# Expert layer by halves of the output, a last pair in two chains, and several steps of the plan moved

## The chip, the cores and the metric

The kernel runs on one core of a Trainium2 chip. The metric is the device time of one execution in microseconds. A NeuronCore has TensorE (PE, its weight loads shown as PEld), VectorE (DVE), ScalarE (ACT), GpSimd (POOL) and SyncE (SP), which here issues most of the DMAs. Matmuls write to PSUM (banks of 128 x 512 float32); ScalarE or VectorE copy from there to SBUF.

## The reference

Three layers, one after the other, on 8 batches of 576 tokens with 8 heads of 64, so 4608 tokens of 512:

```python
kv = einsum('bhsd,bhse->bhde', k, v)
out = einsum('bhsd,bhde->bhse', q, kv)
out = out / sqrt(mean(out * out, -1) + 1e-6) * g_norm      # linear attention, x = [4608, 512]

h = x @ w_in                                               # [4608, 2048]
x = (h * cos(h)) @ w_out                                   # [4608, 512]

logits = x @ phi                                           # [4608, 32]: 8 experts of 4 slots
d = softmax of logits over the tokens                      # slot_input = d.T @ x
slot_out[e] = relu(slot_input[e] @ w1[e]) @ w2[e]          # 512 -> 1024 -> 512, 8 experts
return (softmax of logits over the slots) @ slot_out       # [4608, 512]
```

## The kernel before

**Blocks.** The tokens are cut into ten blocks (`SIZES`, L64): blocks 0 to 7 of 512 and blocks 8 and 9 of 256 tokens. For each block j and each of 16 slices f of the hidden layer, `main(j, f)` (L382) makes one PSUM bank `h` with 12 matmuls: the weights and the inputs are split in a high and a low part, and three of the four products are taken. `h * cos(h)` follows in four steps: `turns` (ScalarE, L406), `rest` (VectorE, L409), the cosine (ScalarE, L413) and the product (VectorE, L443), which leaves `gT`. There are three `h` banks. Blocks 8 and 9 put two slices of 256 columns in one bank and run these four steps once for the pair (L1114).

**Logits and slots.** `w_out` isn't multiplied out: `wp = w_out @ phi` is made in four parts (`wp_kk`, `wp_tr`, L332 to L348), and the logits are `wp` times `gT` (`logits`, and `logits2` for pairs of slices in blocks 0 and 1). `gT` is also brought into the other orientation, by TensorE transposes (`gtr`) or by VectorE transposes and DMAs (`regroup`), and multiplied with the softmax weights `d` (`slot_acc`, L612). For block 9 the end of this is a chain: `l_add` (L544, the last slices' part of the logits), `l_max`, `l_exp` (L563), `l_T` (transposes of `ld`, copy to `d`), `last_slots`.

**The next block's inputs.** While block n runs, the inputs of block n + 1 are made in its steps, per tile t of 128 tokens: `att_out` (matmuls, square, reduction, a power on POOL), `att_xs` (scaling), `att_xT` (transposes, copy `hi` on ScalarE) and `att_lo` (the remainder `lo` on VectorE, L253). The first `main` of a block needs all of its tiles.

**The plan.** The order of each engine's work is written out by hand. `at(j, f, fn)` puts a call behind `main(j, f)` (list `side`), `late` behind `rest` (list `post`), `end` behind the product (`fin`), `ld_at` ahead of the step (`loads`). `at2` counts on from one block into the next. Blocks 0 and 1 run interleaved (`L=4`: slice f of block 0 with slice f - 4 of block 1; string `PLAN["two"]`): `s0 m0 ... m1 ... s1`, so what is put at (0, f) runs ahead of `main(0, f)`, and what is put at (1, f - 4) runs behind `main(1, f - 4)` in the same step. In these steps the weights are still being converted (L300 to L326). `PLAN["A"]` gives the steps of `att_out`, `att_xs`, `att_xT` and `att_lo` for the next block.

**The experts.** w1 and w2 are loaded by `fill` calls into buffers as these come free (`todo`, L661, is the order: all of w1, w2 of experts 0 to 3 in 512 columns, then w2 of experts 4 to 7 as two halves of 256 columns). `tail` (L739) makes the slot inputs, then `first_layer(0)` and `(1)` for the two groups of four experts, `h_T`, and the second layer: `second_layer(0)` for group 0 in 512 columns, `second_layer(1, 1)` and `second_layer(1, 2)` for the two halves of group 1. Its loop has eight steps r of four matmuls, and `then` puts calls behind a step. Once a half of the columns is there for both groups, `select` arranges it, and `half_out(h, u)` (u from 0 to 5) multiplies it with the token weights `cT` (made by `c_T(j)`, j from 0 to 11, two per `half_out`), copies three banks and issues an output DMA of 768 KB on SP. The buffers of the last six refills (`w13` to `w15`, in the list `mid`) hold the last rows of w1 and the first rows of w2 of experts 0 and 1 until then.

## Time and profile before

| | us |
|---|---|
| median of 3 runs | 690.12 (689.81 to 691.18) |
| the profiled execution | 689.97 |
| its span, first to last instruction | 688.2 |
| PE busy | 655.5 (95%) |
| VectorE busy | 496.9 (72%) |
| ScalarE busy | 332.2 (48%) |
| mean granted clock of TensorE | 0.987 |

A line of the timeline gives the start and the duration of an instruction, or of several alike that follow each other (x24), and in brackets how long its engine had been idle and what ended that. Matmuls are pipelined, so one ends after the next has begun; for the time that PE spends, starts are compared with starts. A float32 matmul shows as two instructions. The clock is given as a share of 2.4 GHz: 1.00 and 0.50 are its two levels, and a value in between is a mean over a stretch that has both.

### The profile page before, as it was taken

The page shows a single profiled execution, that of the slowest core. Times are in us where ns is not written, and L with a number is a line of the kernel's source. Part 1 is how long each engine was busy: PE and PEld are TensorE (multiplying, and loading weights), DVE is VectorE, ACT ScalarE, POOL GpSimd, SP SyncE. Part 2 cuts the span into 40 slices and gives each one's busy share as a digit, 9 for nine tenths or more (in the row PEclk, how much of TensorE's full clock was granted, in tenths as well). Part 3 has the DMA queues.
Part 4 walks back from the last instruction along what each step waited for, and adds up shares of the span by engine and source line. Part 5 has one row for each costly group of instructions (what it writes and reads, how often), then busy time and mean ns, then how long its engine had stood idle before and what let it go on. Part 6 is the DMA issues. An engine that isn't in the chain of part 4 may idle for free.

```text
span 688.2 us, 12481 instructions
## 1 busy us (share of the span) xinstructions
PE 655.5 (95%) x4556; PEld 481.2 (70%) x4556; DVE 496.9 (72%) x893; ACT 332.2 (48%) x587; POOL 218.1 (32%) x329
## 2 busy tenths in 40 slices
PE   6879999999999999999999999999999999989994
PEld 6767776875667776767677677767767778874364
DVE  3899987966577778878887888788876656444153
ACT  3675764644354454445445544553554354551143
POOL 3361111211074343540633253245324505001400
PEclk9999999999999999999999999999999999999995
DMA  9945562112186636784777277486635459999978
GB/s 327 363 155 183 198 220 94 57 62 77 51 204 156 172 77 169 202 238 118 167 214 211 70 193 231 120 225 168 150 94 116 103 165 352 334 403 406 373 288 345
DMA packets 72893, 135.12 MB, mean 196 GB/s; under 512 B 11008, under 2 KB 38784, under 8 KB 72320
## 3 DMA queue, kind: packets, MB, share of 16 engines
q1 hardware_dynamic: 65664, 119.63, 54.1%
q0 software_dynamic: 7168, 14.69, 9.1%
q8 instruction: 36, 0.59, 0.4%
q14 instruction: 25, 0.20, 0.1%
HBM read 91.29 MB, written 13.63 MB: 152 GB/s over the span
## 4 chain that ended last, share of the span: by engine, by line
PE 81%; DVE 8%; ACT 5%; issue 2%; DMA 2%; POOL 1%; SPq 0%; DVEq 0%; ACTq 0%; POOLq 0%
PE h L390 50%; PE ab L612 4%; PE ops L203 4%; PE l L515 4%; PE kvps L184 2%; PE eo L792 2%; PE eh L765 2%; PE xTps L240 2%; PE l L524 2%; PE fo L817 2%; PE tr L484 1%; DVE gT L443 1%; ACT tmp L413 1%; PE lr L540 1%; DMA kv<-in_kv 1%
## 5 line engine op out<-in xcount | busy, mean ns | idle before, releaser
L390 PE MATMUL h<-xt,w 128*128 128x512 f32 (+1 forms) x1920 | 422.0, 374 | 6.5 <-DVE xt L253 2.7
L390 PEld LDWEIGHTS h<-xt,w 128*128 128x128 f32 x1920 | 330.1, 189 | 92.1 <-issue 15.2
L413 ACT ACTIVATE tmp<-tmp,hpi 128x512 f32<-128x512 f32 x144 | 104.0, 723 | 174.3 <-DVE tmp L409 174.2
L503 POOL DMA_DIRECT2D g<-tr x224 | 123.4, 554 | 95.5 <-DVE tr L462 50.2
L443 DVE TENSOR_TENSOR gT<-tmp,h 128x512 f32<-128x512 f32 x131 | 89.8, 686 | 70.6 <-ACT tmp L413 70.5
L215 POOL TENSOR_TENSOR ri<-ss,mhalf 128x8 f32<-128x8 f32 x36 | 59.6, 1660 | 210.2 <-DVE ss L213 205.3
L409 DVE SCALAR_TENSOR_TENSOR tmp<-h,tmp 128x512 f32<-128x512 f32 x144 | 97.0, 677 | 22.8 <-ACT tmp L406 22.1
L406 ACT ACTIVATE tmp<-h 128x512 int32<-128x512 f32 x144 | 85.0, 590 | 51.0 <-PE h L390 50.8
L462 DVE STREAM_TRANSPOSE tr<-gT 128x512 f32<-128x512 f32 x103 | 73.3, 711 | 6.4 <-DMA g<-tr 1.6
L326 POOL TENSOR_TENSOR w<-st_m,w 128x512 fp32r<-128x512 f32 x16 | 21.4, 1338 | 72.1 <-ACT w L321 72.1
L203 PE MATMUL ops<-kvA,q 128*128 128x128 f32 (+1 forms) x320 | 38.4, 279 | 0.0
L244 ACT ACTIVATE xt<-xTps,gn 128x512 fp32r<-128x512 f32 x36 | 24.4, 683 | 28.3 <-PE xTps L240 28.3
L203 PEld LDWEIGHTS ops<-kvA,q 128*128 128x128 f32 (+1 forms) x320 | 34.4, 180 | 3.0 <-issue 2.2
L253 DVE SCALAR_TENSOR_TENSOR xt<-xTps,gn,xt 128x512 fp32r<-128x512 f32 x36 | 26.1, 730 | 7.6 <-ACT xt L244 7.3
L210 ACT ACTIVATE sq<-ops 128x512 f32<-128x512 f32 x32 | 19.0, 595 | 25.6 <-PE ops L203 25.3
L612 PE MATMUL ab<-g,d 128*32 128x512 f32 x256 | 31.3, 593 | 0.0
L515 PE MATMUL l<-gT,wp 128*32 128x512 f32 (+1 forms) x248 | 30.2, 556 | 0.0
L212 DVE TENSOR_REDUCE ss<-sq 128x8 f32<-128x512 f32 x32 | 21.6, 675 | 8.0 <-ACT sq L210 7.8
L184 PEld LDWEIGHTS kvps<-kv 128*64 128x64 f32 x448 | 15.4, 137 | 11.7 <-issue 8.7
L222 DVE TENSOR_TENSOR sq<-ops,ri 128x512 f32<-128x512 f32 x32 | 21.5, 677 | 2.3 <-POOL ri L215 2.3
L240 PE MATMUL xTps<-ident,sq 128*128 128x128 f32 x128 | 19.7, 278 | 3.4 <-DVE sq L222 3.4
L612 PEld LDWEIGHTS ab<-g,d 128*32 128x32 f32 x256 | 8.9, 110 | 18.6 <-issue 16.8
(184 smaller groups left out, 633.6 us busy)
## 6 DMA issues: line engine op xcount, KB each, us to landing
kv<-in_kv SPq DMA_DIRECT2D x28, 512.0 KB, 5.3
g<-tr SPq DMA_DIRECT2D x224, 64.0 KB, 3.6
g<-tr POOLq DMA_DIRECT2D x224, 64.0 KB, 3.8
q<-in_qT SPq DMA_DIRECT2D x36, 256.0 KB, 5.9
out<-ot SPq DMA_DIRECT2D x12, 768.0 KB, 4.1
ew<-in_w SPq DMA_DIRECT2D x17, 512.0 KB, 10.3
rw<-in_w_in SPq DMA_DIRECT2D x16, 512.0 KB, 4.4
nat<-in_w_out SPq DMA_DIRECT2D x16, 512.0 KB, 3.9
```

Of the source, the lines that this page charges most:

```text
L203: nc.tensor.matmul(out=ps[p0:p0 + n, pr * 128:(pr + 1) * 128], lhsT=q_t[j, t][:, pr, p0:p0 + n], rhs=kvbd[b % 2][:, pr, :], start=True, st ...
L215: nc.gpsimd.tensor_tensor(out=ri[:, :, 0], in0=ss, in1=mhalf, op=ALU.pow)
L240: nc.tensor.transpose(ps[:, kk * 128:(kk + 1) * 128], xs[:, kk * 128:(kk + 1) * 128], ident)
L390: nc.tensor.matmul(out=ps, lhsT=w[:, a, kk, :], rhs=x[b][:, kk, :], start=(n == 0), stop=(n == 3 * KD - 1))
L406: nc.scalar.activation(out=t.bitcast(I32), in_=ps, func=AF.Copy, bias=0.25, scale=INV_2PI)
L409: nc.vector.scalar_tensor_tensor(out=t, in0=ps, scalar=INV_2PI, in1=t.bitcast(I32), op0=ALU.mult, op1=ALU.subtract)
L413: nc.scalar.activation(out=t, in_=t, func=AF.Sin, bias=hpi, scale=TWO_PI)
L443: nc.vector.tensor_tensor(out=g, in0=fr, in1=h_t.pop((j, f)), op=ALU.mult)
L462: nc.vector.transpose(out=tr_t[j, q][:, :, i, :], in_=gT_t[j, n * q + i].rearrange("p (b t) -> p b t", t=32))
L503: (nc.gpsimd if b % 2 else nc.sync).dma_start(out=dst[32 * b:32 * b + 32, :, x, a:a + n, :].rearrange("p t f i -> p t (f i)"), in_=src[32 ...
L515: nc.tensor.matmul(out=l_t[j][32 * o:32 * o + 32, :], lhsT=wp[:, f, :], rhs=gT_t.pop((j, f)), start=(c == 0), stop=(c == (2 if j == NB - 1 ...
L612: nc.tensor.matmul(out=ps[32 * c:32 * c + 32, :], lhsT=d[:, t, :], rhs=gs[c // 2][t][:, (c % 2) * 512:(c % 2) * 512 + 512], start=(t == 0) ...
```

## The change

In the plan of block 1, `att_out` of block 2's third and fourth tile goes from steps 12 and 13 to 11 and 12, their `att_xT` from 14 and 15 to 13 and 14. In block 8, the second tile of block 9 has its `att_xT` in step 13 instead of 15. `logits2(1, 4)` goes from (0, 11) to (1, 7), and `logits2(1, 12)` from (1, 15) to (1, 17), which is (2, 1). The last pair of slices of block 9 gets two banks and two chains of 256 columns. The copy of the raw logits for the token weights goes from `l_exp` to `l_T`, `l_raw` to just before `c_softmax`. The second layer runs group 0 in halves too: half 1 of both groups, then half 2 of group 0 with two `half_out` in it, then half 2 of group 1 with two more. The very last output goes out in three DMAs of 256 KB.

```diff
--- before.py
+++ after.py
@@ -48,7 +48,7 @@
     lT=20,
     sa=22,
     A=(((1, 1, 2, 2), (1, 1, 1, 1), (2, 2, 3, 3), (0, 1, 1, 0)),
-       ((9, 10, 12, 13), (0, 0, 0, 0), (11, 12, 14, 15), (0, 0, 0, 0))),
+       ((9, 10, 11, 12), (0, 0, 0, 0), (11, 12, 13, 14), (0, 0, 0, 0))),
     K=((0, (0, 0, 0, 0)), (1, (1, 3, 5, 7)), (1, (13, 15, 17, 19))),
     KL=(((0, 1), (1, 2), (1, 4), (1, 6)), ((1, 11), (1, 14), (1, 16), (2, 2))),
     ao=(2, 5, 8, 11),
@@ -396,7 +396,7 @@
 
     def exp_table():
         t = sm_p.tile([128, 2], F32, tag="sb", name="et")
-        nc.scalar.activation(out=t[:, 0:1], in_=m_run, func=AF.Exp, scale=0.0)
+        nc.scalar.activation(out=t[:, 0:1], in_=mhalf[:, 0:1], func=AF.Exp, scale=0.0)
 
     def cos_a(j, f):
         fr_tt(j, f)
@@ -417,7 +417,7 @@
         return tmps[tmp_n[0] % 2]
 
     def fr_tt(j, f):
-        fr_t[j, f] = tmp_one()
+        fr_t[j, f] = tmp_one()[:, 0:h_t[j, f].shape[-1]]
         turns(fr_t[j, f], h_t[j, f])
 
     def round_off(j, f):
@@ -437,9 +437,18 @@
         ring.append([(j, f)] + r[1:])
         return r[1]
 
+    last_g = []
+
     def cos_c(j, f):
         fr = fr_t.pop((j, f))
-        g = ring_next(j, f)
+        g = last_g.pop() if last_g else ring_next(j, f)
+        if (j, f) in ((NB - 1, NF - 2), (NB - 1, NF - 1)):
+            if f % 2 == 0:
+                last_g.append(g[:, 256:512])
+                g = g[:, 0:256]
+            gT_t[j, f] = g
+            nc.vector.tensor_tensor(out=g, in0=fr, in1=h_t.pop((j, f)), op=ALU.mult)
+            return
         nc.vector.tensor_tensor(out=g, in0=fr, in1=h_t.pop((j, f)), op=ALU.mult)
         if j >= SMALL:
             gT_t[j, f], gT_t[j, f + 1] = g[:, 0:256], g[:, 256:512]
@@ -562,9 +571,7 @@
         sb = sm_p.tile([128, 2], F32, tag="sb", name="sb")
         nc.scalar.activation(out=ld, in_=ps, func=AF.Exp, bias=mb[:, 2:3], accum_out=sb[:, 0:1])
         if j == NB - 1:
-            lraw = we[:, 512:512 + SIZES[j]]
-            nc.vector.tensor_copy(out=lraw[0:32], in_=ps[0:32])
-            ls_t[j] = lraw
+            ls_t[j] = ps
         else:
             nc.vector.tensor_copy(out=ld[0:32], in_=ps[0:32])
         if j:
@@ -588,7 +595,11 @@
         nc.vector.tensor_copy(out=d, in_=ps[:, 0:TT[j], 32:64])
         if not tok:
             tok.append(const.tile([128, NT, NS], F32, tag="l_tok", name="l_tok"))
-        if j < NB - 1:
+        if j == NB - 1:
+            lraw = we[:, 512:512 + SIZES[j]]
+            nc.vector.tensor_copy(out=lraw[0:32], in_=ls_t[j][0:32])
+            ls_t[j] = lraw
+        else:
             nc.vector.tensor_copy(out=tok[0][:, T0[j]:T0[j] + TT[j], :], in_=ps[:, 0:TT[j], 0:32])
         d_t[j] = d
 
@@ -784,17 +795,17 @@
         so = [a_p.tile([128, 512], F32, tag="a", name="so") for _ in range(2)]
         st_all = one_p.tile([128, 2, 256], F32R, tag="ls", name="st")
 
-        def second_layer(G, h=0, then={}):
-            n = 256 if h else 512
-            ps = (at_bank("eo") if h == 2 else ps_m.tile([128, 512], F32, tag="h", name="eo"))[:, 0:n]
+        def second_layer(G, h, then={}):
+            ps = (at_bank("eo") if h == 2 else ps_m.tile([128, 512], F32, tag="h", name="eo"))[:, 0:256]
+            c = (h - 1) * 256
             for r in range(8):
                 for i in range(4):
+                    w = GR[i, 1, 0, r][:, c:c + 256] if G == 0 else GR.pop((4 + i, 1, h, r))
                     nc.tensor.matmul(out=ps[32 * i:32 * i + 32, :], lhsT=hT[G][0][:, r, 32 * i:32 * i + 32],
-                                     rhs=GR.pop((4 * G + i, 1, h, r)), start=(r == 0), stop=(r == 7))
+                                     rhs=w, start=(r == 0), stop=(r == 7))
                 for fn, *a in then.get(r, ()):
                     fn(*a)
-            c = max(h - 1, 0) * 256
-            nc.scalar.copy(out=so[G][:, c:c + n], in_=ps)
+            nc.scalar.copy(out=so[G][:, c:c + 256], in_=ps)
 
         def select(h):
             cc = slice(256 * (h - 1), 256 * h)
@@ -817,12 +828,17 @@
                     nc.tensor.matmul(out=ps[:, 256 * x:256 * x + 256], lhsT=cT_t[j][0:96, t, :], rhs=st[0:96],
                                      start=True, stop=True)
                 (nc.vector.tensor_copy if (3 * u + v) % 2 else nc.scalar.copy)(out=ot[:, 512 * v:512 * v + 512], in_=ps)
-            nc.sync.dma_start(out=out[h - 1, u], in_=ot.rearrange("p (q c) -> p q c", c=256))
+                if (h, u) == (2, 5):
+                    nc.sync.dma_start(out=out[1, 5, :, 2 * v:2 * v + 2],
+                                      in_=ot[:, 512 * v:512 * v + 512].rearrange("p (q c) -> p q c", c=256))
+            if (h, u) != (2, 5):
+                nc.sync.dma_start(out=out[h - 1, u], in_=ot.rearrange("p (q c) -> p q c", c=256))
 
         def two(pool, tag):
             t = pool.tile([128, 2, 1536], F32, tag=tag, name="ot")
             return [t[:, 0], t[:, 1]]
 
+        l_raw(NB - 1)
         c_softmax()
         first_layer(0)
         relu(0)
@@ -840,19 +856,18 @@
         h_T(0, 0)
         h_T(0, 1)
         c_T(0)
-        second_layer(0, then={0: [(c_T, 1)], 1: [(h_T, 1, 0)], 3: [(h_T, 1, 1)]})
-        second_layer(1, 1)
+        second_layer(0, 1, then={0: [(c_T, 1)], 1: [(h_T, 1, 0)], 3: [(h_T, 1, 1)], 5: [(c_T, 2)], 7: [(c_T, 3)]})
+        second_layer(1, 1, then={3: [(c_T, 4)]})
         half = {1: (select(1), two(g_p, "g1") + [gt_p.tile([128, 1536], F32, tag=f"gt{i}", name="ot") for i in (1, 0)]
                     + two(g_p, "g0"))}
-        for u in range(2):
-            c_T(2 * u + 2)
-            c_T(2 * u + 3)
-            half_out(1, u)
-        second_layer(1, 2, then={2: [(c_T, 6), (c_T, 7), (half_out, 1, 2)], 5: [(c_T, 8), (c_T, 9), (half_out, 1, 3)]})
+        second_layer(0, 2, then={2: [(half_out, 1, 0)], 6: [(half_out, 1, 1)]})
+        for j in range(5, 8):
+            c_T(j)
+        second_layer(1, 2, then={0: [(half_out, 1, 2)], 3: [(c_T, 8)], 4: [(half_out, 1, 3)], 6: [(c_T, 9)]})
         half[2] = (select(2), [t_p.tile([128, 1536], F32, tag="T2", name="ot")] + two(g_p, "g1")
                    + [gt_p.tile([128, 1536], F32, tag="gt1", name="ot")] + two(g_p, "g0"))
+        c_T(10)
         half_out(1, 4)
-        c_T(10)
         c_T(11)
         half_out(1, 5)
         for u in range(6):
@@ -916,7 +931,12 @@
         if j < 2:
             for f in range(0, NF, 2):
                 late_in = j and f + 3 + L >= NF - (L < 6)
-                at2(*((1, f + 3) if late_in else (0, max(f + 3 + L, 9) if j else PLAN["l0"][f // 2])), logits2, j, f)
+                if not j:
+                    at2(0, PLAN["l0"][f // 2], logits2, j, f)
+                elif f == 4 or late_in:
+                    at2(1, 17 if f == 12 else f + 3, logits2, j, f)
+                else:
+                    at2(0, max(f + 3 + L, 9), logits2, j, f)
         if j < NB - 1:
             for c in range(4 * (j > 1)):
                 at2(j, 4 * c + 7 if j == SMALL else PLAN["lg"][c], logits, j, c)
@@ -944,8 +964,6 @@
         at2(j, lT, l_T, j)
         at2(j, sa, slot_acc, j)
         end2(j, sa, slot_add, j)
-        if j == NB - 1:
-            at2(j, sa, l_raw, j)
 
     for b in range(1, B):
         p, i = divmod(b, 2)
@@ -961,7 +979,7 @@
         if n < 2:
             ao, dx, xt, dl = PLAN["A"][n]
         elif n == SMALL:
-            ao, dx, xt, dl = (5, 9), (2, 2), (9, 15), (0, 0)
+            ao, dx, xt, dl = (5, 9), (2, 2), (9, 13), (0, 0)
         for t in range(TT[j]):
             i = T0[j] + t + 3
             if i < NT:
@@ -1112,6 +1130,19 @@
             cos_c(j, f)
             run(fin, j, f)
         for j, f in [(j, f) for j in range(SMALL, NB) for f in range(0, NF, 2)]:
+            if (j, f) == (NB - 1, NF - 2):
+                for i in range(2):
+                    ps = ps_m.tile([128, 512], F32, tag="h", name="h")[:, 0:256]
+                    run(loads, j, f + i)
+                    main(j, f + i, ps)
+                    run(side, j, f + i)
+                    if i:
+                        cos_b(j, f)
+                    cos_a(j, f + i)
+                cos_c(j, f)
+                cos_b(j, f + 1)
+                cos_c(j, f + 1)
+                continue
             ps = ps_m.tile([128, 512], F32, tag="h", name="h")
             for i in range(2):
                 run(loads, j, f + i)
```

## Rows read from the trace of the kernel before

**Rows 1.** Page, part 1: busy time of each engine, share of the span, instructions.

```profile
PE 655.5 (95%) x4556; PEld 481.2 (70%) x4556; DVE 496.9 (72%) x893; ACT 332.2 (48%) x587; POOL 218.1 (32%) x329
```

**Rows 2.** Waits of PE, whole span: total us, times, longest.

```profile
PE l L524 <- ACT wp L347: 2.6, 1, 2.6
...
PE h L390 <- DVE xt L253: 2.7, 4, 1.3
```

**Rows 3.** Timeline of PE from 100: start, duration (us), work, [idle before <- releaser].

```profile
104.40 1.06 PE L524 MATMUL l<-st,wp 128*32 128x512 f32 x1 [2.63 <-ACT wp L347]
...
106.25 6.35 PE L390 MATMUL h<-xt,w 128*128 128x512 f32 x24
...
114.29 1.05 PE L524 MATMUL l<-gT,wp 128*32 128x512 f32 x4
...
115.27 5.74 PE L390 MATMUL h<-xt,w 128*128 128x512 f32 x24
```

**Rows 4.** Stretches: us, busy by engine (instructions), granted clock, DMA share, GB/s.

```profile
100.00:110.00 10.00, 7.37 (x31) 4.65 (x30) 7.83 (x13) 4.74 (x11) 1.27 (x1) 0.83 0.57 191
```

**Rows 5.** Timeline of DVE, same stretch.

```profile
110.55 0.69 DVE L409 SCALAR_TENSOR_TENSOR tmp<-h,tmp 128x512 f32<-128x512 f32 x1 [1.36 <-ACT tmp L406]
...
113.27 0.69 DVE L409 SCALAR_TENSOR_TENSOR tmp<-h,tmp 128x512 f32<-128x512 f32 x1 [2.03 <-ACT tmp L406]
...
121.68 0.69 DVE L409 SCALAR_TENSOR_TENSOR tmp<-h,tmp 128x512 f32<-128x512 f32 x1 [1.26 <-ACT tmp L406]
```

**Rows 6.** Timeline at the end of block 1.

```profile
168.01 0.42 PEld L240 LDWEIGHTS xTps<-ident,sq 128*128 128x128 f32 x4
...
170.63 1.67 PE L390 MATMUL h<-xt,w 128*128 128x512 f32 x6 [0.69 <-DVE xt L253]
```

**Rows 7.** Timeline at the end of block 8.

```profile
571.95 0.68 DVE L222 TENSOR_TENSOR sq<-ops,ri 128x512 f32<-128x512 f32 x1
...
576.22 0.43 PEld L240 LDWEIGHTS xTps<-ident,sq 128*128 128x128 f32 x4 [0.41 <-issue]
...
578.44 5.90 PE L390 MATMUL h<-xt,w 128*128 128x256 f32 x47 [0.40 <-DVE xt L253]
```

**Rows 8.** Timeline at the end of block 9.

```profile
609.04 0.42 DVE L534 COPY ls<-l 128x256 f32<-128x256 f32 x1
...
611.46 0.69 DVE L409 SCALAR_TENSOR_TENSOR tmp<-h,tmp 128x512 f32<-128x512 f32 x1 [2.00 <-ACT tmp L406]
...
613.68 1.13 PE L544 MATMUL lr<-gT,we 128*128 128x256 f32 x4 [1.93 <-DVE gT L443]
...
615.75 0.47 ACT L563 ACTIVATE ld<-lr,mb 128x256 f32<-128x256 f32 x1 [1.33 <-DVE mb L555]
```

**Rows 9.** Timeline of PE in the tail.

```profile
642.41 1.06 PE L792 MATMUL eo<-ew,hT 128*32 128x512 f32 x8
...
643.40 0.54 PE L730 MATMUL cT<-ident,cs 128*96 128x128 f32 x3
...
651.47 1.91 PE L792 MATMUL eo<-kv,hT 128*32 128x256 f32 x32
...
655.03 1.23 PE L803 MATMUL sel<-so,sel 128*96 128x256 f32 x4
...
657.19 0.77 PEld L817 LDWEIGHTS fo<-st,cT 96*128 96x128 f32 x6 [0.53 <-DVE st L807]
```

**Rows 10.** Timeline of SP: the fifth and the sixth of twelve output DMAs.

```profile
669.34 0.33 SPq L820 DMA_DIRECT2D out<-ot  x1
...
671.75 0.33 SPq L820 DMA_DIRECT2D out<-ot  x1
```

**Rows 11.** Stretches near the end; columns as in rows 4.

```profile
670.00:675.00 5.00, 4.41 (x25) 3.59 (x26) 3.78 (x6) 2.93 (x5) 0.00 (x0) 0.92 0.89 363
...
675.00:680.00 5.00, 4.66 (x19) 4.01 (x18) 3.25 (x6) 2.92 (x5) 0.00 (x0) 0.50 1.02 412
```

**Rows 12.** DMA issues by line: engine, count, KB each, median us to landing.

```profile
ew<-in_w2h SPq DMA_DIRECT2D x18, 256.0 KB, 7.7
```

## The prediction, made before the change was run

> **What bounds the kernel now.** I read the page first: PE is busy for 95% of the span [rows 1], so nothing is worth a microsecond unless it takes time off PE's own queue, or lies in one of the few stretches where PE waits. So the second view is the list of PE's waits. Two of its entries lie where this change works: 2.6 us for the copy of `wp`, once, and 2.7 us in four waits for VectorE's half of the transposed inputs `xt` [rows 2]. The timelines around them say what each really costs, which is more than the wait itself. Two stretches have other limits. Around 100 to 120 us VectorE is nearly full, because the weights are still being converted there, so PE's gain has to be checked against VectorE. From 671.75 us to the end the DMA engines carry a backlog of outputs at a share of 1.02 [rows 10, 11], and there the end is set by when the sixth output is issued, not by PE.
>
> **Logits of a pair, from step (0,11) to (1,7).** PE reached `logits2(1, 4)` straight after the transposes that make `wp`, and waited 2.63 us for ScalarE's copy, which stood behind other work in ScalarE's queue. The pair then ran at the lower of PE's two clock levels: the granted clock of 100 to 110 us is 0.83, that is, some 3.4 us at 1.2 instead of 2.4 GHz [rows 4], and the slow rows stand right behind that wait. So the pair took 106.25 - 104.40 = 1.85 us against 115.27 - 114.29 = 0.98 for a pair at full clock, and the 24 matmuls after it 6.35 against 5.74 [rows 3]. In the new place PE goes on with the 24 matmuls, 5.5 us of cover for the copy. Gain: 2.63 + 0.87 + 0.61 = 4.1 us. VectorE has to follow: in the same steps it idles 1.36 + 2.03 + 1.26 = 4.65 us waiting for ScalarE, which waits for PE [rows 5], so there is just enough slack for 4.1. If VectorE gave back only its first two idles less one hand-over (3.39 - 1.4), 2.0 us would be left. Bounds 2.0 and 4.2; I take 4.1, since the idle rows exceed it. What comes late next is VectorE, with half a microsecond to spare. The pair (1,12) moves from step (1,15) to (2,1): the same 0.98 us of PE on either side of the block's boundary, zero.
>
> **Attention steps of block 2, one step earlier.** The last `att_xT` of block 2 stood in step (1,15), directly ahead of the first matmul of block 2, which needs its ScalarE copy and then its VectorE remainder. PE's weights for the transposes are in by 168.01 + 0.42 = 168.43, and the stream of `h` really goes on at 170.63; one matmul of 0.23 ran in between. That is 1.97 us lost [rows 6]. Moved to (1,14), the copy and the remainder have a whole step, 2.8 us, and the other work of (1,15) as cover. If that cover were gone, the old 1.97 would be back. `att_out` of two tiles moves with it, with its square, reduction, power on POOL and scaling; these go from steps (1,12) and (1,13) to (1,11) and (1,12), and VectorE's `att_xs` there stands behind the previous pair's products, so POOL's power delays nothing of PE. The q loads behind them on SP go one step earlier and wait for the same readers. Gain 2.0; bounds 1.3 (the waits alone, with some of them left) and 2.0.
>
> **Block 9's second tile, from step (8,15) to (8,13).** The same pattern: weights in at 576.22 + 0.43 = 576.65, stream again from 578.44, one matmul of 0.12 in between: 1.67 us lost [rows 7]. At the new place the transposes may wait themselves: `att_xs` ends at 571.95 + 0.68 = 572.63, and PE gets there 24 matmuls of 0.125 and a group of logits before 576.22, at about 572.7. So a stall of up to 0.2 us. On ScalarE the copy now stands ahead of `turns` of pair (12,13) and pushes that chain by a microsecond, but its bank is needed only three microseconds later. Gain 1.6; bounds 1.0 and 1.7.
>
> **Last pair in 256 columns.** The old chain after the last matmul ran in 512 columns, and PE waited 1.93 us for its product; then it had four matmuls (1.13 us) before VectorE could take the maximum [rows 8]. In halves, the first half's steps run before the second's last matmul has come out, and behind the second half only one of the two products is left for PE. A 256-column step costs 0.42 on VectorE and 0.47 on ScalarE against 0.69 for 512 [rows 8]. After the old start of `rest` (611.46) the new order has: rest 0.42, cosine 0.47, product 0.42 with three hand-overs, 1.4 us, against 2.22 to PE's start; but that `rest` starts 0.3 us later, because on ScalarE the first half's cosine goes ahead of the second half's `turns`. So 0.5 us earlier, and half of 1.13 off behind it: 1.05, of which some 0.15 is lost again, because PE's warm-up matmuls and the last transposes then end later than `ld`. Moving the copy `lraw` behind `d` gives 0.05. Gain 0.9; bounds 0.3 and 1.1. Reading `mhalf` instead of `m_run` for the table load: the load sat in an idle of 1.33 us of ScalarE [rows 8], zero.
> The Trainium skill (VectorE: DVE Perf Modes, section The TRN2 errata) speaks against this edit: small operations pay a fixed cost each, so tiles should have at least 512 elements. The rows agree that two halves cost more than one whole, 0.84 against 0.69 on VectorE. By that rule alone this term would be a loss of 0.3 and the sum 684.4; but the engine idles 2.00 us in front of `rest` [rows 8], so here a latency is paid and not occupancy.
>
> **`l_raw` later.** Its two small transposes ran while PE had to wait for `part` anyway; now they stand just ahead of the first layer. Three larger transposes take 0.54 [rows 9], so between 0 and 0.4; I take 0.2 of loss. The softmax of c starts 0.6 later and feeds POOL's splits, which have microseconds to spare.
>
> **The second layer by halves.** No matmul is saved. A 512-column step that stands alone takes 643.40 - 642.41 = 0.99 us; in 256 columns eight steps take 655.03 - 651.47 = 3.56, 0.445 each [rows 9]. So a lone step costs 0.1 for changing over, and the transposes around it as much. The new order cuts the stretch from 642.41 to the sixth output into some 13 more pieces: 1.3 to 1.9 us, I take 1.6. What it gives: the first select comes 1.4 us earlier, since half of expert group 0 is put off, and its wait (PE idle 0.53 before `fo` [rows 9]) is covered by the put-off half. The first outputs are therefore issued some 1.5 us earlier, but they meet an idle queue, and nothing follows from that. The sixth output comes 1.6 - 0.5 = 1.1 later than 671.75, at 672.85. The fifth comes at about 671.4 instead of 669.34, because the put-off half and `c_T(10)` now stand ahead of it [rows 10]. From there on the queue never runs empty: 768 KB at 412 GB/s are 1.9 us each [rows 11]. Old: seven transfers from 671.75. New: eight from 671.4, so the end moves by 1.9 - 0.35 = 1.55; by the sixth alone it would be 1.1. The last output in three DMAs of 256 KB is zero to 0.2 of loss: its first parts can be issued earlier, but they stand behind four outputs. Together 1.6 of loss; bounds: a gain of 0.5 (changing over hidden, first select's gain kept) and a loss of 2.5.
> A new wait: the last six loads of w2 refill buffers that hold the first rows of expert group 0, which are now read again in the second half's steps 0 to 3. SP stands at these refills until about 657, and the first outputs are queued behind them on SP; before, these loads had been released by then. The expert group 1 steps that read them come some 9 us later, and such a load took 7.7 from issue to landing [rows 12]: covered, with little to spare.
>
> **Sum.** -4.1 - 2.0 - 1.6 - 0.9 + 0.2 + 1.6 = -6.8. The profiled execution took 689.97 (span 688.2 and 1.8 around it), 0.15 from the median of 690.12, so 683.2.
>
> **The rivals.**
> First, VectorE sets the pace at 110 to 140 us and only 2.0 of the 4.1 arrive: 685.3. For it: VectorE's slack exceeds the gain by 0.5 only. Against it: all of its idles in these rows are waits that lead back to PE.
> Second, the tail costs nothing, as the changing over is hidden and the first select's gain is kept: 681.3. For it: PE takes weights ahead of time; against it: the lone step of 0.99.
> Third, the refill comes late: if a load takes 12 us from issue instead of 7.7, expert group 1's last steps wait 3 us and the output with them: 686.2.
> Fourth, slower than before: the tail's many short groups let PE's clock fall early. In this trace it fell after one wait of 2.6 us, and in the tail between 670 and 675, where the granted clock is 0.92 and then 0.50 [rows 11]. PE has 14 us of work from 656 to 670; at the lower level from 656 on, the sixth output comes 13 us later, 696. It decides from a fall before about 663, where 7 us are added. Against it: the new order leaves PE fewer waits there than before.
> The Trainium skill (TensorE: Matmul & The Clock Gate, section A second HAM failure mode: psum-queue depth-cycling) describes this: short idles between groups that cycle through PSUM banks make the clock swing. No row before 670 in the tail shows it.
>
> **How the numbers follow.** Forecast 683.2 (own range 682.0 to 684.5): 0.52. VectorE-bound 685.3: 0.15. Tail free 681.3: 0.18. Late refill 686.2: 0.10. Clock, slower: 0.05. The range runs from the free tail with the upper gains (680.9) to the late refill (686.3). Faster by over 0.2% (about what a measurement of this kernel can tell from no change): all but the clock case and a corner of small gains, 0.93; the same 0.02; slower 0.05.
>
> **What would show it.** PE without a wait for `wp`, and the clock at 1.00 from 100 to 110; no wait of `h` for `xt` at the starts of blocks 2 and 9; a last pair whose PE wait is under 1.2 us; the first output some 10 us earlier on the clock than before, the fifth only some 6.3; the DMA share above 1 from there to the end. The prediction is wrong if VectorE shows no idle at all from 110 to 140 while PE waits, or if the distance from the second layer's start to the end shrinks.

## The result, and the profile after

The changed kernel takes 684.28 us (median; 683.31 to 686.16), the kernel before, run beside it, 690.36 (689.81 to 691.18): a ratio of 0.9914, 95% interval 0.9891 to 0.9938, so 4.3 to 7.5 us faster. The forecast was 683.2, with a range of 680.9 to 686.3. The profiled execution of the changed kernel took 683.31 with a span of 681.5; before it was 689.97 and 688.2. The two spans differ by 6.65 us, and this is where PE gained and lost them:

| start of | before | after | earlier by |
|---|---|---|---|
| 17th slice of 160 in PE's order | 95.05 | 95.37 | -0.32 |
| 25th slice, behind the moved pair | 130.66 | 126.62 | 4.04 |
| block 3 | 237.34 | 231.52 | 5.82 |
| block 7 | 484.46 | 478.68 | 5.78 |
| block 8 | 541.55 | 535.34 | 6.21 |
| 9th slice of block 9 | 592.91 | 585.13 | 7.78 |
| slot inputs | 620.12 | 611.29 | 8.83 |
| second layer | 642.41 | 633.57 | 8.84 |
| fifth output issued | 669.34 | 662.78 | 6.56 |
| sixth output issued | 671.75 | 664.18 | 7.57 |
| end | 688.15 | 681.50 | 6.65 |

The first line is a start that was 0.32 later; nothing ahead of it was changed, and in the fourteen profiled executions of this document that slice starts anywhere from 94.92 to 96.08. So up to the second layer the change gains 9.16 us, and from there to the end it loses 2.19. The first output was issued 9.18 earlier (649.65 instead of 658.83; forecast some 10), the fifth 6.56 (forecast 6.3).

The page of the changed kernel, busy time of each engine:

```profile
PE 655.6 (96%) x4620; PEld 482.1 (71%) x4620; DVE 497.1 (73%) x895; ACT 332.9 (49%) x590; POOL 218.1 (32%) x329
```

PE's busy time is the same as in [rows 1], with 64 instructions more for the halves; the kernel with the halves alone is busy for 657.6. So in net all that was gained is idle time. PE's waits, whole span (total us, times, longest):

```profile
PE h L390 <- DVE xt L253: 1.6, 2, 1.3
...
PE lr L553 <- DVE gT L450: 0.7, 1, 0.7
...
PE fo L828 <- DVE cT L742: 0.2, 1, 0.2
```

The wait for `wp` of [rows 2] is gone, and of the four for `xt` two are left, both before 53 us, where nothing was changed. No wait for `ew` stands in the list.

PE behind the transposes of `wp`, answering [rows 3]: start, duration, work:

```profile
101.82 0.27 PE L346 MATMUL wpT<-ident,st_m 128*128 128x128 f32 x1
101.85 5.73 PE L390 MATMUL h<-xt,w 128*128 128x512 f32 x24
...
111.23 5.06 PE L390 MATMUL h<-xt,w 128*128 128x512 f32 x21
```

And the stretch of [rows 4] (us, busy by engine, granted clock, DMA share, GB/s):

```profile
100.00:110.00 10.00, 10.00 (x69) 7.65 (x69) 8.65 (x14) 6.29 (x14) 1.30 (x1) 1.00 0.54 183
```

PE's next matmul starts 0.03 us behind the start of the last transpose. PE fills all ten microseconds, and the clock stays at its upper level. The group that began at 115.27 now begins at 111.23 (its row shows 21 of the 24, as the view ends at 116). VectorE follows; its idle time there has shrunk to one piece of 0.71, where [rows 5] had 1.36, 2.03 and 1.26:

```profile
117.64 0.69 DVE L409 SCALAR_TENSOR_TENSOR tmp<-h,tmp 128x512 f32<-128x512 f32 x1 [0.71 <-ACT tmp L406]
```

The starts of blocks 2 and 9, answering [rows 6, 7], have no bracket left, so no wait:

```profile
163.40 0.29 PE L187 MATMUL kvps<-vr,kz 128*64 128x64 f32 x4
163.62 1.66 PE L390 MATMUL h<-xt,w 128*128 128x512 f32 x6
```

```profile
569.98 0.64 PE L524 MATMUL l<-gT,wp 128*32 128x256 f32 x8
570.55 2.66 PE L390 MATMUL h<-xt,w 128*128 128x256 f32 x20
```

The last pair, answering [rows 8]. PE's wait is 0.69 instead of 1.93, although `rest` of the second half still idles 1.85 for ScalarE:

```profile
603.86 0.43 DVE L409 SCALAR_TENSOR_TENSOR tmp<-h,tmp 128x256 f32<-128x256 f32 x1 [1.85 <-ACT tmp L406]
...
604.67 1.37 PE L553 MATMUL lr<-gT,we 128*128 128x256 f32 x4 [0.69 <-DVE gT L450]
```

The tail, answering [rows 9]. PE in the second layer, a lone step of 256 columns (x8: four matmuls), a run of four such steps, and the fifth output's group:

```profile
633.57 0.64 PE L804 MATMUL eo<-ew,hT 128*32 128x256 f32 x8
634.14 0.53 PE L741 MATMUL cT<-ident,cs 128*96 128x128 f32 x3
...
640.39 1.93 PE L804 MATMUL eo<-kv,hT 128*32 128x256 f32 x32
642.26 0.53 PE L741 MATMUL cT<-ident,cs 128*96 128x128 f32 x3
...
659.42 1.23 PE L814 MATMUL sel<-so,sel 128*96 128x256 f32 x4
660.50 0.49 PE L741 MATMUL cT<-ident,cs 128*96 128x128 f32 x3
660.74 0.97 PE L828 MATMUL fo<-st,cT 96*128 96x256 f32 x6
```

The lone step takes 634.14 - 633.57 = 0.57, one in a run (642.26 - 640.39) / 4 = 0.47: each change-over costs 0.1, as [rows 9] had it. The issues of the fifth and sixth output, and the stretches behind them (columns as above), answering [rows 10, 11]:

```profile
662.78 0.33 SPq L835 DMA_DIRECT2D out<-ot  x1
...
664.18 0.33 SPq L835 DMA_DIRECT2D out<-ot  x1
```

```profile
660.00:665.00 5.00, 4.62 (x29) 3.67 (x28) 3.55 (x6) 3.29 (x7) 0.00 (x0) 1.00 0.53 216
665.00:670.00 5.00, 4.83 (x24) 3.98 (x22) 3.62 (x7) 3.13 (x6) 0.00 (x0) 0.78 1.02 408
670.00:675.00 5.00, 1.82 (x8) 1.38 (x6) 1.93 (x3) 1.27 (x3) 0.00 (x0) 0.50 1.02 415
```

From 665 on, two microseconds behind the fifth issue, the DMA engines are full. In the tail the clock falls only after 665.

### The profile page after: what moved, and what is told of

The parts are those of the page before. It is cut to its first block, busy times and chain, and to the rows that moved or that the text cites. A ratio compares the mean times of both kernels' runs of the same rounds, so it can differ in the third digit from the quotient of the medians.

```text
span 681.5 us, 12625 instructions
## 1 busy us (share of the span) xinstructions
PE 655.6 (96%) x4620; PEld 482.1 (71%) x4620; DVE 497.1 (73%) x895; ACT 332.9 (49%) x590; POOL 218.1 (32%) x329
## 4 chain that ended last, share of the span: by engine, by line
PE 80%; DVE 7%; ACT 4%; DMA 3%; issue 2%; SPq 1%; POOL 0%; ACTq 0%
PE h L390 50%; PE ab L623 4%; PE ops L203 4%; PE l L524 4%; PE xTps L240 2%; PE eh L776 2%; PE kvps L184 2%; PE tr L493 2%; PE l L533 2%; PE eo L804 1%; PE fo L828 1%; DVE gT L452 1%; ACT tmp L413 1%; PE lr L549 1%; DMA out<-ot 1%
## 5 line engine op out<-in xcount | busy, mean ns | idle before, releaser
L413 ACT ACTIVATE tmp<-tmp,hpi 128x512 f32<-128x512 f32 (+1 forms) x145 | 104.3, 720 | 172.5 <-DVE tmp L409 172.3
L409 DVE SCALAR_TENSOR_TENSOR tmp<-h,tmp 128x512 f32<-128x512 f32 (+1 forms) x145 | 97.1, 673 | 18.2 <-ACT tmp L406 17.2
L406 ACT ACTIVATE tmp<-h 128x512 int32<-128x512 f32 (+1 forms) x145 | 85.3, 588 | 44.4 <-PE h L390 44.0
L210 ACT ACTIVATE sq<-ops 128x512 f32<-128x512 f32 x32 | 19.1, 597 | 22.1 <-PE ops L203 21.8
```

The costliest lines, as they stand in the source:

```text
L406: nc.scalar.activation(out=t.bitcast(I32), in_=ps, func=AF.Copy, bias=0.25, scale=INV_2PI)
L409: nc.vector.scalar_tensor_tensor(out=t, in0=ps, scalar=INV_2PI, in1=t.bitcast(I32), op0=ALU.mult, op1=ALU.subtract)
L413: nc.scalar.activation(out=t, in_=t, func=AF.Sin, bias=hpi, scale=TWO_PI)
```

## The experiments

Ratios are to the kernel before in the same comparison, with 95% intervals; a hundredth is 6.9 us.

**The logits pairs alone.** From the kernel before:

```diff
+                elif f == 4 or late_in:
+                    at2(1, 17 if f == 12 else f + 3, logits2, j, f)
...
```

> The kernel before with the moved logits pairs alone. Theory (the pair only waited, and VectorE has slack): PE goes on with the matmuls of h behind the transposes, the wait for wp is gone, the granted clock from 100 to 110 is 1.00, and the time falls by 4.2 us (3.9 to 4.5), as the starts of the changed kernel show in that stretch (4.04, and 4.35 net of a start that was 0.31 later). Rival (VectorE sets the pace from 110 to 140): only some 2.0 of it reach block 2, and PE waits there for gT or h.

Measured: 0.9976 (0.9963 to 0.9990), 1.7 us faster instead of 4.2. PE's starts in the profiled execution do gain what was expected: the 25th slice starts at 126.18 instead of 130.66, and the wait for `wp` is gone. But block 2 gives it back. The start of block 2:

```profile
163.98 0.49 PE L390 MATMUL h<-xt,w 128*128 128x512 f32 x1 [0.78 <-ACT xt L244]
166.15 5.10 PE L390 MATMUL h<-xt,w 128*128 128x512 f32 x15 [1.67 <-DVE xt L253]
```

and the stretch around it:

```profile
164.00:174.00 10.00, 8.33 (x30) 5.85 (x32) 6.74 (x15) 6.40 (x9) 0.00 (x0) 0.83 0.11 45
```

against before:

```profile
164.00:174.00 10.00, 8.37 (x51) 5.03 (x50) 7.00 (x15) 5.96 (x9) 0.00 (x0) 1.00 0.16 53
```

The wait for `xt` is 1.67 instead of 0.69 [rows 6], and the granted clock is 0.83, so part of the stretch ran at the lower level, where before shows 1.00. The gain of 4.48 at the 25th slice has shrunk to 2.26 at the 35th. Another 1.4 goes at the last pair, where this trace has a granted clock of 0.86. So VectorE doesn't set the pace (the rival falls: PE waits for neither `gT` nor `tmp`), but the theory's price isn't reached either. Two suspects: the other pair, (1,12), and the clock.

**The inputs of blocks 2 and 9 alone.** 

```diff
-       ((9, 10, 12, 13), (0, 0, 0, 0), (11, 12, 14, 15), (0, 0, 0, 0))),
+       ((9, 10, 11, 12), (0, 0, 0, 0), (11, 12, 13, 14), (0, 0, 0, 0))),
...
-            ao, dx, xt, dl = (5, 9), (2, 2), (9, 15), (0, 0)
+            ao, dx, xt, dl = (5, 9), (2, 2), (9, 13), (0, 0)
```

> The kernel before with the earlier input steps of block 2 and of block 9's second tile alone. Theory (each removes a stall of PE that stands by itself): 1.8 off at the start of block 2 and 1.6 at the start of block 9, 3.3 us in all (3.0 to 3.6). Rival (in the changed kernel part of this came from the stretch ahead of it being shifted by the logits): 2.5 or less, with a wait of h for xt left at one of the two places.

Measured: 0.9954 (0.9938 to 0.9970), 3.2 us faster, and no wait of `h` for `xt` at either place. In the profiled execution 1.78 arrives between the 25th and the 35th slice and 1.57 between the starts of block 8 and of block 9's ninth slice. The theory holds.

**The last pair alone,** with the later copy and `l_raw`.

```diff
+            if (j, f) == (NB - 1, NF - 2):
+                for i in range(2):
+                    ps = ps_m.tile([128, 512], F32, tag="h", name="h")[:, 0:256]
...
+        l_raw(NB - 1)
         c_softmax()
```

> The kernel before with the last pair of slices in two chains of 256 columns, the raw-logits copy behind d and the later l_raw alone. Theory (a latency is paid there, not occupancy): 1.0 us off at the slot inputs' start, l_raw costs in its new place what it gave in the old one, and the time falls by 1.0 (0.7 to 1.3). Rival (two small operations cost more than one): no gain, or up to 0.3 us of loss.

Measured: 0.9986 (0.9976 to 0.9996), 1.0 us faster. The slot inputs start 1.06 earlier, measured from the last slice; the tail's first matmul loses 0.23 of it where `l_raw` went, and gains 0.23 where it had been. The theory holds.
The Trainium skill (VectorE: DVE Perf Modes, section The TRN2 errata) asks for tiles of at least 512 elements, since each small one pays a fixed cost; by that this edit should lose. Here each half does pay it (0.42 us against 0.69 for a whole), but VectorE idles in front of the second half, and the run decides against the rule for this place:

```profile
612.61 0.42 DVE L409 SCALAR_TENSOR_TENSOR tmp<-h,tmp 128x256 f32<-128x256 f32 x1 [1.85 <-ACT tmp L406]
```

This kernel has the stretch of 100 to 110 as before, with its wait, and shows something else there:

```profile
105.43 0.62 PE L533 MATMUL l<-st,wp 128*32 128x512 f32 x1 [2.63 <-ACT wp L347]
...
106.41 5.74 PE L390 MATMUL h<-xt,w 128*128 128x512 f32 x24
```

```profile
100.00:110.00 10.00, 7.37 (x38) 5.32 (x37) 8.65 (x14) 5.21 (x11) 1.27 (x1) 1.00 0.55 184
```

The same wait of 2.63, but the granted clock is 1.00 and the pair takes 0.98, not 1.85 [rows 3]. From the 17th to the 25th slice PE takes 34.13 here and 35.61 before, so the lower clock cost 1.48. The lower clock behind this wait is not a fixed price of it.

**The second layer by halves alone,** with the last output in three pieces.

```diff
-        second_layer(0, then={0: [(c_T, 1)], 1: [(h_T, 1, 0)], 3: [(h_T, 1, 1)]})
-        second_layer(1, 1)
+        second_layer(0, 1, then={0: [(c_T, 1)], 1: [(h_T, 1, 0)], 3: [(h_T, 1, 1)], 5: [(c_T, 2)], 7: [(c_T, 3)]})
+        second_layer(1, 1, then={3: [(c_T, 4)]})
...
```

> The kernel before with the second layer by halves and the last output in three pieces alone. Theory (more changing over, and the fifth output later, from which the outputs queue up): 2.2 us slower (1.8 to 2.6). Rival one (in the changed kernel the loss came from PE being 8.8 us earlier while the weight loads are not, so that the refills have less cover): 0.8 slower or less, since here the loads have all of their cover. Rival two (the new order is free, and the loss came from somewhere else): within 0.3.

Measured: 1.0030 (1.0018 to 1.0042), 2.1 us slower. From the second layer's first matmul to the end it takes 691.04 - 643.13 = 47.91 us; the changed kernel takes 681.50 - 633.57 = 47.93, and before 688.15 - 642.41 = 45.74. So the loss is a property of the order, the same with PE arriving 9.6 us later (643.13 against 633.57) while the loads have all of their cover, and both rivals fall.

```profile
643.13 0.64 PE L793 MATMUL eo<-ew,hT 128*32 128x256 f32 x8
```

**The changed kernel with the tail of before.**

```diff
+        second_layer(0, then={0: [(c_T, 1)], 1: [(h_T, 1, 0)], 3: [(h_T, 1, 1)]})
+        second_layer(1, 1)
...
```

> The changed kernel with the second layer and the outputs in the order of before (group 0 in 512 columns, one last DMA). Theory (the new order of the tail loses 2.2 us): 8.3 us faster than before, some 682.0 us, which beats the changed kernel. Rival (the new tail is needed because PE reaches it 8.8 us earlier and the loads don't): 6.1 or less faster, with PE waiting for ew or kv in the second layer.

Measured: 681.47 us, 0.9870 (0.9855 to 0.9885), 9.0 us faster than before, and no wait for weights in the second layer. Its interval lies below that of the changed kernel (0.9891 to 0.9938). From the second layer to the end it takes 45.78.

**The fifth output before the second select.**

```diff
+        half_out(1, 4)
         half[2] = (select(2), ...
         c_T(10)
-        half_out(1, 4)
         c_T(11)
```

> The changed kernel with one line moved: the fifth output is made before the second select instead of behind it and c_T(10). Theory (the end is set by the fifth output's issue, eight transfers and no gap): the fifth is issued some 1.5 us earlier, the end is then set by the sixth, and the time falls by 0.5 to 1.0 us against the changed kernel, to about 683.5. Rival (the end is set by a lagging DMA engine or by PE's work up to the seventh output): within 0.2 of the changed kernel.

Measured: 683.83 us, 0.9910 (0.9897 to 0.9923), against 0.9914 of the changed kernel: not told apart by the times. The trace says why. From the second layer's first matmul the fifth is issued after 27.48 us instead of 29.21, but the sixth after 31.15 instead of 30.61, since `c_T(10)` and `c_T(11)` now follow each other and PE waits for the second's copy:

```profile
661.40 0.82 PE L741 MATMUL cT<-ident,cs 128*96 128x128 f32 x6
663.16 0.95 PE L828 MATMUL fo<-st,cT 96*128 96x256 f32 x6 [0.95 <-DVE cT L742]
```

The end comes 16.50 behind the sixth, as before (688.15 - 671.75 = 16.40), and the distance is 47.65 instead of 47.93. Behind the fifth it comes 20.17, where the changed kernel has 18.72: so it isn't the fifth's issue alone that sets the end. The rule that the later of the two sums does holds; the price of this edit was misjudged by that wait.

**The last output in one piece.**

```diff
-                if (h, u) == (2, 5):
-                    nc.sync.dma_start(out=out[1, 5, :, 2 * v:2 * v + 2],
...
-            if (h, u) != (2, 5):
-                nc.sync.dma_start(out=out[h - 1, u], in_=ot.rearrange("p (q c) -> p q c", c=256))
+            nc.sync.dma_start(out=out[h - 1, u], in_=ot.rearrange("p (q c) -> p q c", c=256))
```

> The changed kernel with the last output in one DMA of 768 KB, as before. Theory (the pieces stand behind four outputs in the queue, so their earlier issue gives nothing, and each has its own cost): 0.2 us faster than the changed kernel (0 to 0.5). Rival (the last landing follows the last piece, which is smaller): 0.3 to 0.6 us slower than the changed kernel.

Measured: 684.49 us, 0.9923 (0.9906 to 0.9940). In the trace the distance is 48.32, that is 0.39 longer than with three pieces, so the theory (0 to 0.5 shorter) has no support; the times can't decide.

**Warm-up matmuls in the wait for `wp`.** From the kernel before:

```diff
+                if (j, f) == (1, 4):
+                    at2(0, 11, warm, 10)
```

> The kernel before with ten warm-up matmuls of 128 columns put between the transposes of wp and the logits pair that waits for wp, so that PE isn't idle there; the wait for ScalarE stays. Theory (PE's idle time of 2.6 us is what the lower clock follows): the granted clock from 100 to 110 is 1.00 and the 1.5 us of slow rows behind the wait come back, 1.3 to 1.6 faster than before. Rival (the clock falls there for another reason, or the warm-up matmuls hold a PSUM bank that somebody needs): the slow rows stay, 0 to 0.5 us slower.

Measured: 1.0020 (1.0005 to 1.0034), 1.4 us slower. The clock is 1.00 from 100 to 110, and the 25th slice starts 1.5 earlier, measured from the 17th (34.13 against 35.61), just as in the kernel with the last pair alone. But from 164 to 174, where before had 1.00, it is 0.83: in this execution the lower level shows behind the wait at block 2's start instead. The theory's rows came, its time didn't. As the kernel with the last pair alone kept the upper level with PE idle, the warm-up matmuls can't be credited with it either. Why the median is slower than before stays open.

**Pair (1,4) alone, and pair (1,12) alone.** From the kernel before:

```diff
-at2(*((1, f + 3) if late_in else ...
+at2(*((1, f + 3) if late_in or (j, f) == (1, 4) else ...
```

> The kernel before with the logits pair (1,4) alone moved; (1,12) stays in step (1,15). Theory (with both pairs moved, (1,12) left PE at block 2's start 0.98 us earlier than xt, and the wait for xt grew by as much): block 2's first matmul 4.5 earlier than before, its wait for xt 0.7 as before, not 1.7, and the time about 1.0 us lower than with both pairs, some 2.7 to 4.0 faster than before; how much of that arrives depends on whether the lower clock shows behind another wait instead. Rival (something else in blocks 1 and 2 gives the gain back): 1.7 faster as with both pairs, and the same 1.7 us wait at block 2.

```diff
-at2(*((1, f + 3) if late_in else ...
+at2(*((1, 17 if f == 12 else f + 3) if late_in else ...
```

> The kernel before with the logits pair (1,12) alone moved over the boundary to step (2,1). Theory (the pair was cover for xt, and is now paid for behind the wait): 0.9 slower (0.5 to 1.2), with the wait for xt at block 2 grown from 0.7 to 1.7 us. Rival (0.98 us of PE on either side of the boundary, as the prediction had it): within 0.3.

Measured: (1,4) alone 0.9959 (0.9944 to 0.9974), 2.8 us faster; (1,12) alone 1.0039 (1.0021 to 1.0057), 2.7 us slower. At block 2's start the first has the old wait again, the second the longer one:

```profile
166.20 2.11 PE L390 MATMUL h<-xt,w 128*128 128x512 f32 x8 [0.68 <-DVE xt L253]
```

```profile
170.74 3.51 PE L390 MATMUL h<-xt,w 128*128 128x512 f32 x14 [1.67 <-DVE xt L253]
```

So (1,12) was cover for `xt`: taken away it leaves a longer wait, and has to be paid for behind it. That is shown; in the trace it costs 0.85 up to the 35th slice. The rest of its 2.7 isn't explained by it; its trace loses 1.4 more at the last pair, at a granted clock of 0.86 from 608 to 620.
With (1,4) alone, 4.34 us are kept all through to the last slice (605.40 against 609.74). They fall to 2.8 at the last pair, whose wait of 1.93 still stands there:

```profile
609.34 1.85 PE L544 MATMUL lr<-gT,we 128*128 128x256 f32 x4 [1.93 <-DVE gT L443]
```

```profile
608.00:620.00 12.00, 10.30 (x112) 6.76 (x116) 4.03 (x15) 4.42 (x12) 0.52 (x1) 0.86 1.04 397
```

The four matmuls take 1.85 instead of 1.13 [rows 8], at a granted clock of 0.86 in the stretch. Before has 1.00 there:

```profile
608.00:620.00 12.00, 9.66 (x117) 7.44 (x109) 5.08 (x15) 6.01 (x16) 0.00 (x0) 1.00 1.04 398
```

**A better tail.** The changed kernel with the tail of before and one swap; the second run has the three pieces too.

```diff
         half_out(1, 4)
         c_T(10)
         c_T(11)
+        half_out(2, 0)
         half_out(1, 5)
-        for u in range(6):
+        for u in range(1, 6):
```

> The changed kernel with the second layer and the outputs in the order of before, and the first output of the second half made ahead of the first half's last one, so that it covers PE's wait of 0.9 us for the last cT. Theory (the end is set by the sixth issue, and then by the fifth): the sixth is issued 0.9 earlier, the distance from the second layer's first matmul to the end falls from 45.8 to 45.3, and the time is 0.5 below that of the kernel without the swap, some 9.3 us below before. Rival (the outputs' queue is paced by its slowest DMA engine whatever is issued when): 45.8 as without the swap.

> The same with the last output in three pieces as well. Theory (in the changed kernel the one-piece form ended 0.4 later from the second layer's start): 0.2 to 0.4 below the kernel with the swap alone, a distance of some 45.0 us. Rival (the pieces stand behind four outputs and give nothing): within 0.1 of it.

Measured: 682.23 us, 0.9875 (0.9848 to 0.9901), and 682.20 us, 0.9873 (0.9851 to 0.9895). In the traces the distance from the second layer to the end is 45.31 and 45.24, against 45.78 without the swap: the swap's half microsecond is there as forecast, the pieces give 0.07. The medians can't show either: 682.2 against 681.47, with intervals that cover each other. All three beat the kernel before by 8.6 to 9.0 us and, by their medians, the changed kernel by 2 to 3. Only for the one without the swap does the interval lie wholly below the changed kernel's; the traces have all three 2.1 to 2.7 shorter from the second layer to the end.

## Why the prediction was right, step by step

**The logits pair, -4.1.** In the whole change 4.04 arrived at the 25th slice, 4.36 net of the later start, for the reason given. The VectorE rival is refuted by the profile of both kernels that have the move. But 1.48 of the term (0.87 + 0.61, the slow rows) is not a fixed price: the kernel with the last pair alone had the same wait at the upper clock. The step that took this part from one execution as certain was wrong, and that the execution compared had it was a matter of chance: of the five profiled kernels with this wait, four show 0.83 from 100 to 110 and one 1.00.

**The pair (1,12), zero.** Wrong by itself: alone it costs 0.85 in the trace, as the wait behind it grows by as much as it had covered. In the whole change it costs nothing, because the inputs are there earlier: from the 25th to the 35th slice PE takes 45.63 in the changed kernel and 45.77 with the inputs alone.

**The inputs.** Block 2: forecast -2.0, measured from the 25th to the 35th slice -1.92 in the whole change (47.55 to 45.63) and -1.78 alone. Up to block 3 it is -1.78 (5.82 - 4.04) and -1.30, but the rest of block 2, where nothing was changed, takes 58.7 to 60.4 in the fourteen profiled executions. Block 9: -1.6, measured -1.57 (7.78 - 6.21), alone -1.57. The feared stall of 0.2 did not show.

**The last pair.** -0.9, measured -1.06 up to the second layer (8.84 - 7.78), alone -1.06.

**`l_raw`.** +0.2, measured 0: it gave back in the old place what it costs in the new one. The step that let its two transposes hide behind the wait for `part` was wrong.

**Not forecast.** 0.39 between block 3 and block 8 (5.82 to 6.21), nearly all of it in block 7, where PE waits 0.33 for `ls` (L534) before, and not after. It reads as scatter and not as a gain of the change: the same wait is absent with the inputs alone, with the warm-up matmuls and with the swap, and stands with 0.29 to 0.32 in the other four variants of the changed kernel.

**The second layer by halves.** +1.6, measured 2.19 (45.74 to 47.93), within its bounds. The mechanism was as described: the fifth output 2.28 later from the second layer's start (forecast 2.06), the sixth 1.27 (forecast 1.1), and a queue of eight transfers from the fifth. Mis-sized was the last term: from the fifth it took 18.72, from the old sixth 16.40, so here the eighth transfer cost 2.3 and not 1.9. That is no fixed price: where the fifth set the end, it took from 18.3 (with the swap) to 19.1 (in one piece), that is 1.9 to 2.7 for the eighth. In the kernel before, the end stood 18.81 behind the fifth as well, so from the two kernels alone the fifth's delay by itself would explain the loss; the run with the fifth first shows that the sixth counts too. The late refill did not show: SP issued the last one at 649.11, and no step waited for it. The fourth rival, an early fall of the clock, did not come: from 660 to 665 it is 1.00.

The Trainium skill (TensorE: Matmul & The Clock Gate, section A second HAM failure mode: psum-queue depth-cycling), cited for that rival, has short idles between groups swing the clock; in this tail, with more and shorter groups than before, no row up to 665 shows it.

**The sum.** For the profiled execution: -4.04 - 1.78 - 0.39 - 1.57 - 1.06 + 2.19 = -6.65, as measured; the forecast was -6.8. The median lies 1.0 above that execution. That the sum is so close is in part luck: the tail cost 0.6 more than forecast, and the 0.39 of scatter and 0.36 from the last pair and `l_raw` made up for it.

The rival of a free tail doesn't follow from its terms: without the loss of 1.6 the sum gives 681.6, with the full gain of 0.5 681.1, not 681.3.

**The parts don't add up.** Alone, by the ratios, they give -1.7 - 3.2 - 1.0 + 2.1 = -3.8, together -5.9. Part of the gap is the pair (1,12): with (1,4) alone in place of both pairs the parts give -4.9. The five intervals together leave some 2.4 either way (an estimate, from the root of their squares), so the gap of 2.1 isn't clear of the noise. The traces show one thing that can widen it: every drop of the granted clock between 100 and 620 us stands at one of three waits of PE (for `wp`, at block 2's start, at the last pair), but there isn't a drop behind each.

| kernel | 100 to 110 | 164 to 174 | 608 to 620 |
|---|---|---|---|
| before | 0.83 | 1.00 | 1.00 |
| both pairs alone | 1.00 | 0.83 | 0.86 |
| (1,4) alone | 1.00 | 1.00 | 0.86 |
| (1,12) alone | 0.83 | 1.00 | 0.86 |
| inputs alone | 0.83 | 1.00 | 1.00 |
| last pair alone | 1.00 | 1.00 | 1.00 |
| second layer by halves alone | 0.83 | 1.00 | 1.00 |
| warm-up matmuls | 1.00 | 0.83 | 1.00 |
| changed kernel and its five variants | 1.00 | 1.00 | 1.00 |

Only the kernels of the last line have none of the three waits at their old length. Where the wait for `wp` was taken away or covered, all three traces have a drop behind a later wait; with the last pair alone there is none at all, with (1,12) alone there are two. By wait, the drop came in four of five executions behind the one for `wp`, in two of seven at block 2's start and in three of seven at the last pair. One execution of each kernel is too little for a rate, and that a drop moves on to the next wait is not shown.

## What to carry to other kernels

Price a removed wait by the wait itself, and book a lower clock behind it as a chance, not a sum: one profile shows one execution. Before moving work over a boundary, ask what it covered there, and move the producer first. Where a queue of outputs sets the end, count from each issue (the later of "fifth plus eight transfers" and "sixth plus seven") before reordering the engine that feeds it: here the end came 16.4 to 16.5 us behind the sixth or 18.3 to 19.1 behind the fifth, whichever was later, and the old order of the tail was better by 2 to 3 us.

## What the runs showed of the hardware

The lower clock follows a wait of PE only in some executions: the same wait of 2.63 us stood at a granted clock of 0.83 in one kernel and of 1.00 in another with the same code up to there, and made a difference of 1.48 us. The clock differs from one execution to the next at other places too: from 15 to 25 us, where no kernel was changed, it is 0.83 in seven of the fourteen profiled executions and 1.00 in the others.

A full queue of outputs does not drain at one rate. In the changed kernel's landing times the sixth output came in over 1.66 us from the first to the last of the sixteen DMA engines, in the kernel before over 0.18, and with the second layer by halves alone over 1.65. All four kernels with the new tail show 1.26 to 2.02 there, the ten with the old order of the second layer 0.15 to 0.22. That two outputs are issued close together isn't enough for it: with the swap they are 1.14 apart, nearer than in the changed kernel (1.40), and the spread is 0.22. What slows single engines was not tested.
